# Causal mask by select instead of by product, one normalization for two heads, and output products moved by one slot in a fused attention and feed-forward kernel

## The chip, the cores and the metric

One core of a Trainium2 chip runs the whole program. The metric is the device time of one execution in microseconds (us); less is better. The engines work side by side, each through its own instructions in the order written: TensorE (PE in the profile; PEld its weight loads), VectorE (DVE), ScalarE (ACT), GpSimd (POOL), and SyncE (SP), which only issues transfers.

## What is computed

Attention over 8 batches of 8 heads, 576 positions, 64 values a head, with a causal mask and a bias from a running sum, and then a feed-forward layer on the 4608 rows of 512.

```python
scores = (q @ k.T) / sqrt(64)
s_pos = maximum(s, 0); cum = cumsum(s_pos)
bias = -(cum[query] - cum[key])
scores = where(key > query, -1e9, scores + minimum(bias, 0))
attn = exp(scores - max); attn = attn / (sum(attn) + 1e-9)
x = attn @ v                            # heads side by side: 4608 x 512
h = x @ w_in                            # 512 x 2048
out = (h * clip(h + 3, 0, 6) / 6) @ w_out   # 2048 x 512
```

## The kernel before

**Pairs and slots.** The 64 heads go by in 32 pairs, numbered from 0; four pairs (PPB) make a batch. One turn of the loop over `p` (L847) is called a slot here. For each head, `scores` makes three banks of 512 scores, keys on partitions: g = 0 holds the four blocks on the diagonal, g = 1 and 2 the blocks off it, and `corner` holds the last 64 keys of both heads. ScalarE takes the exponential of each bank into P and PC (L422, L462). `av` multiplies P with v in two parts: part 0 five blocks off the diagonal, part 1 the rest, ten products; v has a column of ones, so that column 64 of the result is the sum. `norm` takes the reciprocal of that column (L503) and multiplies (L504), which makes the head's half of x. `transpose_x` transposes x on TensorE (L518) and VectorE copies it to xT (L523); from pair 8 on, but for one pair and the last, a transfer does this.

**Operands ahead.** In slot p, `get(0)` and `get(1)` transpose q and k of pair p + 1 on TensorE (L253, L266) into a bank each and copy them into the pair's qk tile, by even and odd positions. Of k, ScalarE copies a part and VectorE the rest (L292, L310). For pairs 3 to 6 (`mixed`) q is kept in another order within blocks of 64, and x is put right by a permuted identity. Rows 64 to 67 of a qk tile hold the terms of the bias, loaded by `load_aug` (L162). Four qk tiles take turns.

**The mask.** For pairs 0 to 7 (NPROD) a product of an identity and a matrix of large negative values (L377; L441 in `corner`) starts the bank. For pairs 8 on, GpSimd sets what lies above the diagonal to zero after the exponential (`shut_out`, L426), and 60 more rows of the qk tile (68 to 127, a coarse staircase) keep the exponentials there in range; they are copied from `stair_sb` by GpSimd (`set_stair`, L695) in slots 5 to 7, and by ScalarE in slots 8 and 9 for the fourth tile.

**The feed-forward layer.** `m1` makes h (L547), ScalarE and VectorE make the activation from it (L562, L563), and `m2` makes the output (L574), which VectorE scales (L590). `group` issues one piece of this, four matmuls of 512 columns; a written plan says which through slots 4 to 16 or so, rules after that. It starts in slot 4, when the first batch's x is there. Its weights are loaded by GpSimd in four and eight pieces (L170, L178) from slot 2 to 7.

**Banks.** Eight banks: two for scores, two for h (used for scores too in the first batch), one `o` for the products of head 0, two `po` that are shared by products of head 1, transposes of k and x, and later the output, and one `t` for the transposes of q and k.

**What sets the order.** The schedule is written by hand: each engine takes its instructions in the order in which the code issues them. In slots 0 to 3 the order is scores (p, 0, g = 0 and 1), q of the next pair, scores g = 2, corner, products and norm of (p - 1, head 1), k of the next pair, two banks of head 1 and products part 0 of head 0, the third bank, `transpose_x(p - 1)`, products part 1, norm of (p, head 0). From slot 4 on groups stand between these. GpSimd's queue has in each slot loads, casts of v (L206, L207), selects and copies, one after the other; SP's has the loads of v and later the transposing transfers.

Of the kernel before, what the change touches and what calls it, by code (L numbers as in the profile page):

```python
# [18 lines left out]
def kernel(  # L19
# [31 lines left out]
    VW = 66  # L51
    NROW = 1
    NWARM = (11, 2, 6)
    HALVES = (slice(0, 288), slice(288, SEQ))
# [3 lines left out]

    grp = (np.arange(128) * 61 // 128)[None, :]
    steps_r = np.arange(1, 61)[:, None]  # L60
    stair = np.zeros((128, 2, 128), np.float32)
    stair[68:, 0] = np.where(grp < steps_r, 1.0, 0.0)
    stair[68:, 1] = np.where(grp == steps_r, NEG_BIG, 0.0)
    stair_dram = nc.inline_tensor(stair.astype(np.float16), name="stair")

# [28 lines left out]
    ident2 = keep("ident2", [128, 128], F16)  # L94
    stair_sb = keep("stair_sb", [128, 2, 128], F16)
    bias3 = keep("bias3", [128, 1], F32)
# [62 lines left out]
    def load_aug(p, eng):  # L159
        for hh in range(2):  # L160
# [49 lines left out]
    early = [True]  # L210
    turn = [0]

    def s_bank(shape, name):
# [209 lines left out]

    def shut_out(ap, w):
        part = ap.rearrange("p (t c) -> p t c", c=w)
        nc.gpsimd.affine_select(  # L426
            out=part,
            in_=part,
            pattern=[[0, part.shape[1]], [1, w]],
            compare_op=ALU.is_ge,  # L430
            fill=0.0,
            base=0,
            channel_multiplier=-1,
        )

    def corner(p):
        S = s_bank([128, 2, 64], "Sc")
        by_product = p < NPROD
        rows = slice(0, 68 if by_product else 128)
        if by_product:  # L440
# [29 lines left out]
    def av(p, hh, part):  # L470
        va, pt = vas[p % NVA], Pof(p, hh)
        if part == 0:

            tag = "o" if not hh or NPROD - 1 <= p < NPE - 2 else "po" if p < NPROD else "t"
            O[p, hh] = psum.tile(
                [128, 5, 65], F32, tag=tag, bufs=2 if tag == "po" else 1, name="O"
            )
        o = O[p, hh]
# [11 lines left out]
        else:  # L490
# [5 lines left out]
            block(4, 4, PCs[p % 2][:, c : c + 128], start=False, stop=True)  # L496

    def norm(p, hh):
        o = O.pop((p, hh))
        if hh == 0:  # L500
            X[p] = work.tile([128, 5, 2, D], F16, tag="x", name="x")
        rl = work.tile([128, 5, 1], F32, tag="rl", name="rl")
        nc.vector.reciprocal(out=rl, in_=o[:, :, 64:65])  # L503
        nc.vector.tensor_tensor(  # L504
            out=X[p][:, :, hh, :],
            in0=o[:, :, 0:64],
            in1=rl.to_broadcast([128, 5, 64]),
            op=ALU.mult,
        )
# [182 lines left out]

    def set_stair(i, copy, heads=(0, 1)):
        for hh in heads:
            copy(  # L695
                out=qks[i][64:128, hh, :, 64 * hh : 64 * hh + 640].rearrange(
                    "p i (t c) -> p i t c", c=128
                ),
                in_=stair_sb[64:128, :, None, :].to_broadcast([64, 2, 5, 128]),
            )  # L700

    fill(nc.vector, xT[:, 0, 0:SEQ], 0.0)

    def warm(n):
        W = psum.tile([128, 512], F32, tag="o", name="W")
# [125 lines left out]
    load_v(1, nc.sync)  # L831
    load_aug(2, nc.sync)
    cast_v(0)
    for i in range(2):
# [12 lines left out]
    for p in range(NP):  # L847
# [39 lines left out]
        def pool_end():  # L887
            if p >= NPROD:
                shut_out(PCs[p % 2][:, 0:128], 64)
                shut_out(Pof(p, 1)[:, 0:512], 128)  # L890
            if p >= NPROD and p != 9 and p + 2 < NP:
                if p == 14:
                    cum6(1, nc.gpsimd, whole)
                load_aug(p + 2, nc.gpsimd)

        if p >= PPB:
            for fn, c in {
                4: ((I, 2),),
                5: ((I, 3),),
                6: ((U, 0), (U, 1), (U, 2), (U, 3)),  # L900
                7: ((U, 4), (U, 5), (U, 6), (U, 7)),
            }.get(p, ()):
                fn(c)
        if PPB <= p < NPROD:
            pool_mid()
            if p == 4:
                load_aug(7, nc.gpsimd)
            elif p in (6, 7):
                load_aug(p + 2, nc.gpsimd)
# [6 lines left out]
        if p == 2:  # L916
            nc.sync.dma_start(out=stair_sb, in_=stair_dram.ap())
        if p == 10:
# [12 lines left out]
        if p < PPB:  # L931
            scores(p, 0, 0)
            scores(p, 0, 1)
            get(0)
            scores(p, 0, 2)
            corner(p)
            if p:
                av(p - 1, 1, 0)
                av(p - 1, 1, 1)
                norm(p - 1, 1)  # L940
            get(1)
            scores(p, 1, 0)
            scores(p, 1, 1)
            av(p, 0, 0)
            scores(p, 1, 2)
            if p:
                transpose_x(p - 1)
            av(p, 0, 1)
            norm(p, 0)
            continue  # L950

        if p == PPB:
            early[0] = False
            scores(p, 0, 0)
            av(p - 1, 1, 0)
            av(p - 1, 1, 1)
# [11 lines left out]
        else:  # L968
            scores(p, 0, 0)
            if p >= NPROD:  # L970
                pool_mid()
            get(0)
            group()
            scores(p, 0, 1)
# [10 lines left out]
        corner(p)  # L985
        if p in (8, 9):
            set_stair(3, nc.scalar.copy, (p - 8,))
        elif p == 11:
            new_sum()
            cum1(1, whole)  # L990
# [6 lines left out]
        scores(p, 1, 0)  # L997
        if p >= NPROD:
            pool_end()
        if PPB < p < NPE - 1:  # L1000
# [64 lines left out]
```

## Time and profile before

| | |
|---|---|
| median of 3 runs | 355.29 us (354.62 to 932.81) |
| the profiled execution | 354.79 us, of which the profile's span is 353.1 us |
| TensorE busy | 345.1 us (98%), 2926 matmuls |
| VectorE busy | 230.2 us (65%) |
| ScalarE busy | 224.7 us (64%) |
| GpSimd busy | 169.7 us (48%) |
| mean granted clock of TensorE | 1.00 |
| transfers | 48.35 MB, 137 GB/s over the span |
| mask products: L377 at 512 columns, 16 | 379 ns each |
| select: L426 at 512 columns, 48 | 651 ns each |
| normalization: L503, L504, 64 each | 186 and 492 ns each |

A line of the timeline gives the start and the length in us from the start of the span, the engine, the line of the code, the operation, what it writes and reads, its shape and how many equal ones were merged; in brackets stands how long the engine was idle before it and what ended that. A matmul's length counts from its start to the landing of its result, so that lengths of matmuls in a row overlap; the distance of their starts tells what each costs.

### The profile page before, as it was taken

The numbers are of one execution on the slowest core, as the hardware profiler recorded it, in microseconds if no ns is written. First come the engines' busy times: TensorE is split into PE (matmuls) and PEld (weight loads), VectorE is DVE, ScalarE is ACT, GpSimd is POOL, SyncE is SP. The second block draws the span as 40 slices with busy tenths as digits, with TensorE's granted clock in tenths as the row PEclk, the third lists the DMA queues.
The fourth block names the chain that finished last, engine by engine and source line by source line (L and its number), as shares of the span: only waits on it lengthen the run. The fifth ranks groups of instructions, "written<-read, shape, count | busy, mean of one in ns | idle before, by whom it ended". The sixth has DMA issues, their size and how long they took to land.

```text
span 353.1 us, 7778 instructions
## 1 busy us (share of the span) xinstructions
PE 345.1 (98%) x2926; PEld 191.0 (54%) x2926; DVE 230.2 (65%) x476; ACT 224.7 (64%) x397; POOL 169.7 (48%) x296
## 2 busy tenths in 40 slices
PE   8999999999999999999999999999999999999995
PEld 3775666555555555555555555555555444444442
DVE  7996997676868677666666666757654544544531
ACT  6987896787787667666776666666664334443310
POOL 8977799676778656455555555555310000000000
PEclk9999999999999999999999999999999999999999
DMA  9999999999999999998798959997120100101112
GB/s 164 152 208 209 199 185 182 117 181 196 154 136 100 190 219 188 173 211 186 168 167 198 179 144 197 181 180 164 38 75 14 59 29 34 59 2 59 59 50 72
DMA packets 144782, 48.35 MB, mean 137 GB/s; under 512 B 130648, under 2 KB 139784, under 8 KB 144744
## 3 DMA queue, kind: packets, MB, share of 16 engines
q1 hardware_dynamic: 117112, 37.54, 54.0%
q0 software_dynamic: 27392, 10.03, 24.8%
q8 instruction: 23, 0.38, 0.4%
q10 hardware_dynamic: 240, 0.28, 0.2%
q14 instruction: 15, 0.12, 0.1%
HBM read 37.36 MB, written 9.44 MB: 133 GB/s over the span
## 4 chain that ended last, share of the span: by engine, by line
PE 90%; DVE 4%; ACT 3%; issue 1%; DMA 1%; ACTq 0%
PE po L574 35%; PE ph L547 34%; PE O L481 7%; PE S L403 7%; PE S L388 4%; DVE qk L310 1%; PE pt L266 1%; ACT P L422 1%; DMA s_all<-in_s_dram 1%; DVE x L504 1%; PE ptx L518 1%; PE Sc L454 1%; ACT tr L562 1%; PE S L377 1%; DVE qk L332 1%
## 5 line engine op out<-in xcount | busy, mean ns | idle before, releaser
L563 DVE SCALAR_TENSOR_TENSOR gT<-tr,ph 128x512 f16<-128x512 f32 x144 | 98.9, 687 | 97.6 <-ACT tr L562 96.5
L547 PE MATMUL ph<-xT,w_in_sb 128*128 128x512 f16 x576 | 148.1, 379 | 0.0
L574 PE MATMUL po<-w_out_sb,gT 128*128 128x512 f16 x576 | 145.9, 379 | 0.0
L562 ACT ACTIVATE tr<-ph,bias 128x512 f32<-128x512 f32 x144 | 99.0, 688 | 73.0 <-PE ph L547 70.6
L422 ACT ACTIVATE P<-S 128x512 f16<-128x512 f32 x192 | 111.3, 595 | 37.5 <-PE S L388 22.3
L547 PEld LDWEIGHTS <-w_in_sb 128*128 128x128 f16 x576 | 51.4, 97 | 44.2
L574 PEld LDWEIGHTS <-gT 128*128 128x128 f16 x576 | 50.0, 97 | 46.5 <-issue 0.2
L426 POOL TENSOR_SCALAR_AFFINE_SELECT P<-P 128x512 f16<-128x512 f16 x48 | 31.3, 651 | 44.4 <-ACT P L422 44.4
L403 PE MATMUL S<-qk 68*128 68x448 f16 (+3 forms) x256 | 49.0, 272 | 0.5 <-ACT P L422 0.5
L481 PE MATMUL O<-va,P 128*128 128x65 f16 x896 | 47.9, 193 | 0.3 <-ACT P L422 0.3
L481 PEld LDWEIGHTS <-P 128*128 128x128 f16 x896 | 39.2, 97 | 14.0 <-ACT P L422 0.5
L230 DVE COPY qk<-jt 64x768 f16<-64x768 f16 x84 | 36.8, 439 | 1.2
L403 PEld LDWEIGHTS <-qk 68*128 68x128 f16 x256 | 23.7, 98 | 24.5 <-issue 0.9
L162 POOL DMA_DIRECT2D qk<-rows_of x56 | 32.8, 588 | 1.1 <-PE S L403 0.3
L504 DVE TENSOR_TENSOR x<-O,rl 128x320 f16<-128x320 f32 x64 | 31.5, 492 | 2.2
L590 DVE TENSOR_SCALAR ob<-po 128x512 f32<-128x512 f32 (+1 forms) x36 | 24.3, 676 | 8.3 <-PE po L574 7.6
L388 PEld LDWEIGHTS <-qk 128*128 128x128 f16 (+1 forms) x256 | 18.9, 97 | 14.0 <-DVE qk L310 1.7
L426 POOL TENSOR_SCALAR_AFFINE_SELECT PC<-PC 128x128 f16<-128x128 f16 x24 | 7.0, 293 | 39.9 <-ACT PC L462 39.8
L388 PE MATMUL S<-qk 128*128 128x128 f16 (+1 forms) x256 | 24.8, 219 | 1.0 <-DVE qk L332 0.5
L206 POOL CAST va<-vraw 128x512 f16<-128x512 f32 x32 | 21.0, 656 | 4.7 <-DMA vraw<-in_v_dram 2.4
L310 DVE COPY qk<-pt 64x576 f16<-64x576 f16 x22 | 17.6, 805 | 6.2 <-ACT qk L310 5.9
L202 POOL CAST tok<-raw 128x576 f16<-128x576 f32 x28 | 18.0, 679 | 0.0
(79 smaller groups left out, 201.9 us busy)
## 6 DMA issues: line engine op xcount, KB each, us to landing
out_dram<-ob SPq DMA_DIRECT2D x35, 256.0 KB, 2.0
vraw<-in_v_dram SPq DMA_DIRECT2D x64, 128.0 KB, 4.0
raw<-in_q_dram SPq DMA_DIRECT2D x14, 288.0 KB
raw<-in_k_dram SPq DMA_DIRECT2D x14, 288.0 KB
tok<-in_q_dram POOLq DMA_DIRECT2D x18, 144.0 KB, 5.2
tok<-in_k_dram POOLq DMA_DIRECT2D x18, 144.0 KB, 5.9
w_in_sb<-in_moe_w_in_dram POOLq DMA_DIRECT2D x4, 512.0 KB, 8.5
w_out_sb<-in_moe_w_out_dram POOLq DMA_DIRECT2D x8, 256.0 KB, 7.1
```

What stands on the lines that cost most here:

```text
L162: eng.dma_start(out=qks[p % NQK][64:68, hh, :, 64 * hh : 64 * hh + SEQ], in_=rows_of[g // 32].rearrange("(r g) i t -> g r i t", g=32)[g % ...
L230: copies[par](out=qk[0:64, :, i, 128 * par : 128 * par + 256 * n].rearrange("p h (s two c) -> p h s two c", two=2, c=128)[:, :, :, 0, :], ...
L388: mm(S[:, c], lhsT=kT[rows, c], rhs=qT[rows, c], start=(j == 0 and not by_product), stop=(j == 3 and p >= NROW),)
L403: mm(S[:, c : c + w], lhsT=kT[0:68, 128 * j : 128 * (j + 1)], rhs=qT[0:68, 128 * (j + 1) : SEQ], start=(c == 0), stop=(c != 0 and p >= NROW),)
L422: nc.scalar.activation(out=pt[:, c], in_=S, func=AF.Exp, scale=0.125)
L426: nc.gpsimd.affine_select(out=part, in_=part, pattern=[[0, part.shape[1]], [1, w]], compare_op=ALU.is_ge, fill=0.0, base=0, channel_multip ...
L481: mm(o[:, i, :], lhsT=lhsT, rhs=va[:, hh, j, 0:65], **kw)
L504: nc.vector.tensor_tensor(out=X[p][:, :, hh, :], in0=o[:, :, 0:64], in1=rl.to_broadcast([128, 5, 64]), op=ALU.mult,)
L547: mm(ph, lhsT=w_in_sb[:, kc, ft * 128 : (ft + 1) * 128], rhs=xT[:, kc, n * 512 : (n + 1) * 512], start=(kc == 0), stop=(kc == NKC - 1),)
L562: nc.scalar.activation(out=tr, in_=ph, func=AF.Relu, bias=bias3[:, 0:1])
L563: nc.vector.scalar_tensor_tensor(out=gTs[n][:, ft, :], in0=tr, scalar=6.0, in1=ph, op0=ALU.min, op1=ALU.mult)
L574: mm(po, lhsT=gTs[n][:, ft, t4 * 128 : (t4 + 1) * 128], rhs=w_out_sb[:, ft, :], start=(ft == 0), stop=(ft == NFT - 1),)
```

## The change

Five things are changed together.

1. The mask is a product only for pairs 0 to 3 (NMASK = 4). From pair 4 on GpSimd selects; for the mixed pairs with a pattern of the same order. `pool_mid` and `pool_end`, which issue the selects, now run in all slots from 4 on, after the scores they read.
2. The staircase has 7 rows instead of 60, with steps of 16, and is loaded straight into rows 68 to 74 of the qk tile by SP (`load_stair`, seven loads for pairs 4 to 10). `set_stair` and its copies are gone.
3. Products of heads 0 and 1 go to a tile of two adjacent banks, `OO`, and for pairs 0 to 2 and 4 to 6 one reciprocal of 128x10 and one multiplication of 128x640 (`norm_pair`) take the place of two of each. In the first batch the products of head 0 of a pair move from the end of its own slot into the next one, and `get(1)` moves ahead of the products of head 1. The tile `po` has one bank; the output takes turns between it and the second bank of `OO`. The transposes of x use bank `t`, but for pair 3.
4. q of pairs 7 to 10 is copied in two parts with a group between them.
5. The pieces of the weights are issued after the select and the cast of v, two of w_out already in slot 5 and three in slots 6 and 7 (before: four in slots 6 and 7). Loads of bias rows for pairs 7 to 9 go from GpSimd's queue to SP's.

```diff
+    NMASK = PPB
+    NSTAIR = 7
...
+    def load_stair(p, eng):
+        eng.dma_start(
+            out=qks[p % NQK][68 : 68 + NSTAIR], in_=stair_drams[mixed(p, 0)].ap()
+        )
...
+    OO = psum.tile([128, 2, 512], F32, tag="oo", name="OO")
+
+    def paired(p):
+        return p < PPB - 1 or PPB <= p < NPROD - 1
...
     def t_bank(other, name):
         if not done[2] and other:
-            return psum.tile([128, 640], F16, tag="po", bufs=2, name=name)
+            return psum.tile([128, 640], F16, tag="po", name=name)
         return psum.tile([128, 640], F16, tag="t", name=name)
...
-        by_product = p < NPROD
+        by_product = p < NMASK
         if g == 0:
-            rows = slice(0, 68 if by_product else 128)
+            rows = slice(0, 68 if by_product else 68 + NSTAIR)
...
-    def shut_out(ap, w):
+    def shut_out(p, ap, w):
         part = ap.rearrange("p (t c) -> p t c", c=w)
+        pattern = [[0, part.shape[1]], [1, w]]
+        if mixed(p, 0):
+            part = part.rearrange("p t (g w v) -> p t g w v", w=4, v=16)
+            pattern = [[0, part.shape[1]], [64, w // 64], [1, 4], [4, 16]]
+            if w == 64:
+                part, pattern = part[:, :, 0], [pattern[0]] + pattern[2:]
...
-            tag = "o" if not hh or NPROD - 1 <= p < NPE - 2 else "po" if p < NPROD else "t"
-            O[p, hh] = psum.tile(
-                [128, 5, 65], F32, tag=tag, bufs=2 if tag == "po" else 1, name="O"
-            )
+            if hh and p >= NPE - 2:
+                O[p, hh] = psum.tile([128, 5, 65], F32, tag="t", name="O")
+            else:
+                half = hh if p < NPROD - 1 else 0
+                O[p, hh] = OO[:, half, 0:325].rearrange("p (i c) -> p i c", c=65)
...
+    def norm_pair(p):
+        o = OO[:, :, 0:325].rearrange("p h (i c) -> p h i c", c=65)
+        X[p] = work.tile([128, 5, 2, D], F16, tag="x", name="x")
+        rl = work.tile([128, 2, 5, 1], F32, tag="rl2", name="rl2")
+        nc.vector.reciprocal(out=rl, in_=o[:, :, :, 64:65])
+        nc.vector.tensor_tensor(
+            out=X[p].rearrange("p i h d -> p h i d"),
+            in0=o[:, :, :, 0:64],
+            in1=rl.to_broadcast([128, 2, 5, 64]),
+            op=ALU.mult,
+        )
+
     def norm(p, hh):
+        if paired(p):
+            if hh:
+                norm_pair(p)
+            return
...
-        pt = t_bank(True, "ptx")
+        pt = t_bank(p == PPB - 1, "ptx")
...
         if fq == 0:
-            po = psum.tile([128, 512], F32, tag="po", bufs=2, name="po")
+            if len(pos) % 2:
+                po = OO[:, 1]
+            else:
+                po = psum.tile([128, 512], F32, tag="po", name="po")
...
         def pool_mid():
-            if p >= NPROD:
-                shut_out(Pof(p, 0)[:, 0:512], 128)
+            shut_out(p, Pof(p, 0)[:, 0:512], 128)
             if nxt:
                 cast_v(p + 1)
-            if p in (5, 6, 7):
-                set_stair((p + 3) % NQK, nc.gpsimd.tensor_copy)
+            for fn, c in {
+                4: ((I, 2),),
+                5: ((I, 3), (U, 0), (U, 1)),
+                6: ((U, 2), (U, 3), (U, 4)),
+                7: ((U, 5), (U, 6), (U, 7)),
+            }.get(p, ()):
+                fn(c)
...
             scores(p, 0, 1)
             get(0)
+            if p:
+                av(p - 1, 0, 0)
+                av(p - 1, 0, 1)
             scores(p, 0, 2)
             corner(p)
+            get(1)
             if p:
                 av(p - 1, 1, 0)
                 av(p - 1, 1, 1)
                 norm(p - 1, 1)
-            get(1)
             scores(p, 1, 0)
             scores(p, 1, 1)
-            av(p, 0, 0)
             scores(p, 1, 2)
             if p:
                 transpose_x(p - 1)
-            av(p, 0, 1)
-            norm(p, 0)
+            if p == PPB - 1:
+                av(p, 0, 0)
+                av(p, 0, 1)
+                norm(p, 0)
             continue
...
             scores(p, 0, 0)
-            if p >= NPROD:
-                pool_mid()
-            get(0)
-            group()
+            pool_mid()
+            if NPROD - 1 <= p + 1 < NPE:
+                pt = transpose_in(p + 1, 0)
+                transpose_out(p + 1, 0, pt, pars=(0,))
+                group()
+                transpose_out(p + 1, 0, pt, pars=(1,))
+            else:
+                get(0)
+                group()
...
-        if p in (8, 9):
-            set_stair(3, nc.scalar.copy, (p - 8,))
```

More of the change, by code (lines that the diff above doesn't have):

```diff
@@ L52 @@
     NROW = 1
+    NMASK = PPB
+    NSTAIR = 7
     NWARM = (11, 2, 6)
     HALVES = (slice(0, 288), slice(288, SEQ))
[L59 to L64, printed above, removed]
+    grp = (np.arange(128) // 16)[None, :]
+    steps_r = np.arange(1, NSTAIR + 1)[:, None]
+    under = np.where(grp < steps_r, 1.0, 0.0)
+    equal = np.where(grp == steps_r, NEG_BIG, 0.0)
+    over = under.reshape(NSTAIR, 2, 16, 4).transpose(0, 1, 3, 2).reshape(NSTAIR, 128)
+    stair_drams = []
+    for name, of_q in (("stair", under), ("stairm", over)):
+        stair = np.zeros((NSTAIR, 2, 2, SPAD), np.float16)
+        for hh in range(2):
+            for i, rows in enumerate((of_q, equal)):
+                stair[:, hh, i, 64 * hh : 64 * hh + 640] = np.tile(rows, (1, 5))
+        stair_drams.append(nc.inline_tensor(stair, name=name))
     cpool = ctx.enter_context(tc.tile_pool(name="consts", bufs=1))
@@ L94 @@
     ident2 = keep("ident2", [128, 128], F16)
-    stair_sb = keep("stair_sb", [128, 2, 128], F16)
     bias3 = keep("bias3", [128, 1], F32)
@@ L428, in shut_out @@
             in_=part,
-            pattern=[[0, part.shape[1]], [1, w]],
+            pattern=pattern,
             compare_op=ALU.is_ge,
@@ L437, in corner @@
         S = s_bank([128, 2, 64], "Sc")
-        by_product = p < NPROD
-        rows = slice(0, 68 if by_product else 128)
+        by_product = p < NMASK
+        rows = slice(0, 68 if by_product else 68 + NSTAIR)
         if by_product:
@@ L691 @@
     nc.gpsimd.tensor_copy(out=unmix(perm), in_=mix(ident))
[L693 to L700, printed above, removed]
     fill(nc.vector, xT[:, 0, 0:SEQ], 0.0)
     def warm(n):
-        W = psum.tile([128, 512], F32, tag="o", name="W")
+        W = OO[:, 0]
         for _ in range(n):
@@ L832 @@
     load_aug(2, nc.sync)
+    load_stair(PPB, nc.sync)
     cast_v(0)
@@ L887, in pool_end @@
         def pool_end():
-            if p >= NPROD:
-                shut_out(PCs[p % 2][:, 0:128], 64)
-                shut_out(Pof(p, 1)[:, 0:512], 128)
+            shut_out(p, PCs[p % 2][:, 0:128], 64)
+            shut_out(p, Pof(p, 1)[:, 0:512], 128)
             if p >= NPROD and p != 9 and p + 2 < NP:
@@ L893, in pool_end @@
                     cum6(1, nc.gpsimd, whole)
[L894 to L904, printed above, removed]
-            pool_mid()
-            if p == 4:
-                load_aug(7, nc.gpsimd)
-            elif p in (6, 7):
                 load_aug(p + 2, nc.gpsimd)
@@ L916 @@
         if p == 2:
-            nc.sync.dma_start(out=stair_sb, in_=stair_dram.ap())
+            for i in range(PPB + 1, NPROD):
+                load_stair(i, nc.sync)
+        if p in (4, 6, 7):
+            n = 7 if p == 4 else p + 2
+            if p != 4:
+                load_stair(n, nc.sync)
+            load_aug(n, nc.sync)
+        elif p == 8:
+            load_stair(10, nc.sync)
         if p == 10:
@@ L969 @@
             scores(p, 0, 0)
-            if p >= NPROD:
-                pool_mid()
-            get(0)
-            group()
+            pool_mid()
+            if NPROD - 1 <= p + 1 < NPE:
[6 more added lines that the diff above has]
+                group()
             scores(p, 0, 1)
@@ L985 @@
         corner(p)
-        if p in (8, 9):
-            set_stair(3, nc.scalar.copy, (p - 8,))
-        elif p == 11:
+        if p == 11:
             new_sum()
@@ L997 @@
         scores(p, 1, 0)
-        if p >= NPROD:
-            pool_end()
+        pool_end()
         if PPB < p < NPE - 1:
```

## The prediction

> **What bounds the kernel now.** I count pairs of heads from 0 as the code does; a slot is one turn of the loop over p. First the busy shares on the page: TensorE has nearly all of the span.
>
> ```profile
> PE 345.1 (98%) x2926; PEld 191.0 (54%) x2926; DVE 230.2 (65%) x476; ACT 224.7 (64%) x397; POOL 169.7 (48%) x296
> ```
>
> Matmuls overlap, so that share can hide waits; the starts in the timeline of TensorE cannot. From 34 us on, each matmul starts where the one before leaves off (512 columns every 0.216 us: groups of four, 0.86 apart), and I find less than 1.2 us of lost time in all of 34 to 350 us. There an instruction taken from TensorE is worth its pitch, and one added costs it. Before 34 us it is different. The timeline of TensorE at the starts of slots 2 and 3:
>
> ```profile
> 17.14 0.45 PE L518 MATMUL ptx<-ident,x 128*128 128x128 f16 x5 [0.39 <-DVE x L504]
> ...
> 17.74 0.38 PE L377 MATMUL S<-shut,ident 128*128 128x512 f16 x1
> 18.34 0.40 PE L388 MATMUL S<-qk 68*128 68x128 f16 x4 [0.22 <-DVE qk L310]
> ...
> 21.73 0.38 PE L377 MATMUL S<-shut,ident 128*128 128x512 f16 x1
> 22.16 0.40 PE L388 MATMUL S<-qk 68*128 68x128 f16 x4
> ...
> 25.55 0.38 PE L377 MATMUL S<-shut,ident 128*128 128x512 f16 x1
> 26.13 0.40 PE L388 MATMUL S<-qk 68*128 68x128 f16 x4 [0.20 <-DVE qk L310]
> ```
>
> Each pair's first scores (L388) start when the last copy of its k is written: a loop from pair to pair, of 4.55, 3.82 and 3.97 us (13.79, 18.34, 22.16, 26.13). The loop of slot 2 can be read on ScalarE and then VectorE:
>
> ```profile
> 18.84 1.57 ACT L422 ACTIVATE P<-S 128x512 f16<-128x512 f32 x3 [1.00 <-PE S L388]
> 20.29 0.30 ACT L462 ACTIVATE PC<-Sc 128x128 f16<-128x128 f32 x1
> 20.44 0.81 ACT L310 COPY qk<-pt 64x576 f16<-64x576 f16 x1
> ```
> ```profile
> 20.26 0.20 DVE L503 RECIPROCAL rl<-O 128x5 f32<-128x5 f32 x1
> 20.49 0.49 DVE L504 TENSOR_TENSOR x<-O,rl 128x320 f16<-128x320 f32 x1
> 21.29 0.81 DVE L310 COPY qk<-pt 64x576 f16<-64x576 f16 x1 [0.31 <-ACT qk L310]
> 22.13 0.46 DVE L523 COPY xT<-ptx 128x576 f16<-128x576 f16 x1
> ```
>
> Scores at 18.34, first exponential 0.50 later, three of them and the corner's, then ScalarE's half of the k copy, and only when that ends (21.25) VectorE's half, to 22.10; scores at 22.16. The normalization at 20.26 to 20.98 costs nothing here: VectorE does it while it waits for ScalarE.
>
> **Part 1: products a slot later, one normalization (pairs 0 to 2).** In the new order of VectorE the k copies of a slot come ahead of the normalization, since the transposes of k are now issued before the last products; and at the end of the slot TensorE transposes x ahead of the next pair's mask and scores, in one queue. So the loop gets longer by what used to lie beside it: reciprocal, multiplication of both heads, five transposes and the mask. The multiplication has no row: 128x320 takes 0.492, and the fused step at 128x512 0.687, so 1.02 ns more an element, 0.82 for 640; its bounds are one (0.49) and two (0.98) of the single ones. Start to start of reciprocal and multiplication is 0.22 (18.69 to 18.91); the transposes are 5 x 0.056 = 0.28, the mask 0.22. A start after VectorE ends costs 0.05 (17.09 to 17.14).
>
> Slot 1: pair 1's scores at 13.62 (its k is written at 13.57; before, they also stood behind a product and a mask, 13.79). Exponentials from 14.07; the third waits for its scores, now behind a product of 15 x 0.031, so the corner's ends at 15.85, ScalarE's k copy at 16.33, VectorE's two (0.48 and 0.80) at 17.65, multiplication 17.91 to 18.73, transposes 18.78, mask 19.06, **scores of pair 2 at 19.28** (18.34 before). Slot 2: +0.5 first exponential; the product puts the third 0.13 later; ScalarE's copy 21.45 to 22.26, VectorE's to 23.11, x at 24.18, transposes 24.23, mask 24.51, **pair 3 at 24.73** (22.16). Slot 3: ScalarE's half is the short one (26.90 to 27.38), VectorE's to 28.70, x at 29.77, transposes 29.82, then pair 3's own first product (0.47), no mask, **pair 4 at 30.57** (26.13). That is +4.4 us; with the bounds of the multiplication +3.4 to +4.9. Slot 4 (26.13 to 34.17, 8.04 us) loses 0.27 us of masks, but its second head already waits for an exponential (0.33 before L403 at 32.78), so I give it 7.85. Pair 5 starts at 38.42, **+4.25**.
>
> **Part 2: mask by select.** Eight masks of 512 columns (L377, 0.216) and four corners (L441, 0.055) go: 1.95 us of TensorE. Of these, slot 4's are counted above, and 0.49 a slot remain for pairs 5, 6, 7: 1.46. Part of it is not had, because of the banks: x is now transposed into the bank of the q transposes (there were two others to take turns in). The copy out of it runs late:
>
> ```profile
> 41.35 0.45 DVE L523 COPY xT<-ptx 128x576 f16<-128x576 f16 x1
> ```
>
> It ends at 41.80, behind the k copies and a fused step, and next slot's q transposes started at 41.70; without the masks TensorE is there at about 41.0 and waits to about 41.6, since ScalarE and VectorE come only 0.2 earlier. The same at 48.83 (copy to 48.73). So slots 5 to 7 give 0.6 of 1.46 (bounds 0 and 1.46). The selects go to POOL: 0.65 for 512 columns, 0.29 for the corner, and for the mixed order of pairs 4 to 6 by the two L679 rows (0.29 plain, 0.34 mixed) up to 0.76. POOL's slot 5 is then two q/k issues 1.3, two selects 1.3 to 1.5, casts 0.9, three weight issues 2.25, corner 0.3: 6.0 to 6.3 in 6.6 to 7.1. The select of the corner, behind the weight issues, ends about 43.6; TensorE wants it at 44.7. So nothing, with 1.1 us of room.
>
> **Part 3: what else moves.** The staircase copies go (POOL 6 x 1.25, ScalarE 2 x 1.25); seven small loads on SP (0.58 to issue) take their place, issued a pair or more ahead, three of them with no reader to wait for; six pair-row loads go from POOL (0.59 each) to SP behind the v loads. SP's issues wait for places 8 loads back, and v lands 9 to 12 us after issue at 27 to 31 us; v of pair 7, issued about 33, is there by 46, and its cast is due at 47. Weights now stand behind select and cast: the last w_in at 41.1, landing within 10.1 (33.51 to 43.63 before) for use at 52.8; the last w_out at 56, landing 63.5 for use at 68.8. No stall, but the room falls to 1.5 us. ScalarE without its copies in slots 8 and 9, and q copies split around a group in slots 6 to 9, can save what TensorE lost there, 0.4 at 71.4 us and little more: **-0.4** (0 to -0.5). From slot 10 on, product and output banks alternate as before: 0.
>
> **Sum.** 4.25 - 0.6 - 0.4 = +3.25 on a span of 353.1. The profiled execution took 354.79, 1.7 outside the span, so **358.0**; the median of the runs shown is 355.29, of which this is +0.8%. With all bounds (3.2 to 4.7; 0 to -1.46; 0 to -0.5; POOL 0 to +0.5) 356.0 to 360.0.
>
> **The clock.** TensorE loses up to 1.9 us at a time in slots 1 to 3. In this trace it idled 0.7 us at 8.6 to 9.3 without the granted clock leaving 1.00; the 11 warming matmuls ran at 0.43 a start. [...]
>
> **Rivals.** A, faster: the loop of the first batch does not close over x, because VectorE reaches the normalization while TensorE is still busy; then the waits of before (0.55, 0.38, 0.20, 0.36 at the starts of slots) go with the masks: 354.8 - 1.95 - up to 1.5, so 351.3 to 353. For it: VectorE is busy only 3.6 of 4 us a slot there. Against: in its order the k copies come first and wait for ScalarE. It decides if x is ready by 3.4 us into slot 2. B, slower still: POOL becomes the one that ends last in slots 4 to 7. Its cast waited 2.24 us for a v load at 36.55; such a wait now stands ahead of weights and selects, and beyond 1.1 us of room each us costs one, three times over: 358 + 1 to 4, 359 to 362. Against: the v loads are issued early relative to the later slots. C: the granted clock halves in the first batch, as in the warming matmuls (0.43 against 0.216); 3.6 us of work a slot becomes 7.2, +5: 363 or more. D, the edits of the later slots do nothing: within the sum, 358.4.
>
> **Chances.** Forecast with D 0.67, A 0.17, B 0.12, C 0.04. Range 352.5 to 361.5: the whole of the forecast's own, more than half of A, most of B. About 2% (7 us) is what a measurement of this kernel can tell from no change. Faster by more than that (under 348.2) 0.02: the masks and all waits together are worth 5; slower (over 362.4) 0.06, from C and the end of B; within, 0.92.
>
> **What would show it.** Right: first scores of pairs 2, 3, 4 near 19.3, 24.7, 30.6; before them TensorE idle on the transposes of x, released by the new multiplication of about 0.8; k copies ahead of it, released by ScalarE; q transposes of pair 7 waiting for the copy of x; no wait of TensorE for a select. Wrong: transposes of x without a wait (A), products released by a select (B), a clock under 1.00 (C), or a multiplication far from 0.8.

## The result and the profile after

The changed kernel takes **401.49 us** (median of 4 runs, 400.32 to 403.44) beside 355.03 of the kernel before on the same chip: 1.132 times as long, with an interval of 1.125 to 1.139. The prediction had 358.0 and a range to 361.5. The profiled execution took 400.32 us, with a span of 398.6 (before 353.1).

TensorE is busy for 88% of the span, from 98%, with 12 matmuls fewer. Its line on the page of the changed kernel:

```profile
PE 349.8 (88%) x2914; PEld 193.2 (48%) x2914; DVE 227.5 (57%) x464; ACT 222.1 (56%) x395; POOL 164.7 (41%) x296
```

What TensorE waits for is in the table of waits of the changed kernel: its columns are the waiting engine, tile and line, what it waited for, us in all, how often, and the longest:

```profile
PE OO L615 <- DVE x L542: 33.6, 19, 1.8
...
PE ptx L556 <- DVE x L525: 5.7, 3, 2.0
```

**The first row is the loss.** It is a matmul of the output (L615, `m2`) that waits for a normalization (L542). The timelines of TensorE and of VectorE near the end of a slot in the long even part of the kernel:

```profile
176.90 0.44 PE L503 MATMUL OO<-va,P 128*128 128x65 f16 x9
177.18 0.19 PE L503 MATMUL OO<-va,PC 128*128 128x65 f16 x1
179.19 1.02 PE L615 MATMUL OO<-w_out_sb,gT 128*128 128x512 f16 x4 [1.82 <-DVE x L542]
```
```profile
177.82 0.69 DVE L601 SCALAR_TENSOR_TENSOR gT<-tr,ph 128x512 f16<-128x512 f32 x1 [1.63 <-ACT tr L600]
178.42 0.19 DVE L541 RECIPROCAL rl<-OO 128x5 f32<-128x5 f32 x1
178.64 0.49 DVE L542 TENSOR_TENSOR x<-OO,rl 128x320 f16<-128x320 f32 x1
```

The products of head 0 end in the first half of OO; the output then starts in the second half, and does so only when VectorE has read the first. The same place of the kernel before, on TensorE and on VectorE:

```profile
157.19 0.19 PE L481 MATMUL O<-va,PC 128*128 128x65 f16 x1
157.22 1.03 PE L574 MATMUL po<-w_out_sb,gT 128*128 128x512 f16 x4
```
```profile
158.44 0.19 DVE L503 RECIPROCAL rl<-O 128x5 f32<-128x5 f32 x1
158.66 0.49 DVE L504 TENSOR_TENSOR x<-O,rl 128x320 f16<-128x320 f32 x1
```

There the output starts 0.03 us after the last product, and the normalization ends 1.9 us later, in nobody's way. After the change the distance of these starts is 2.01 us (177.18 to 179.19), 1.98 more than before. This wait of 1.98 us comes 18 times, from pair 18 on in every pair: there the first scores of a pair come every 11.21 us instead of every 9.22. Taking at each place how much later the group starts than the matmul ahead of it lets it, I get 36.7 us in all.

**The first batch.** First scores of pairs 2, 3 and 4 at 19.37, 25.43 and 32.55 (before 18.34, 22.16, 26.13). TensorE, and VectorE in slot 2:

```profile
18.86 0.45 PE L556 MATMUL ptx<-ident,x 128*128 128x128 f16 x5 [1.93 <-DVE x L525]
...
24.50 0.72 PE L556 MATMUL ptx<-ident,x 128*128 128x128 f16 x5 [1.82 <-DVE x L525]
...
31.79 0.45 PE L556 MATMUL ptx<-ident,x 128*128 128x128 f16 x5 [1.99 <-DVE x L525]
```
```profile
22.53 0.80 DVE L326 COPY qk<-pt 64x576 f16<-64x576 f16 x1 [1.29 <-ACT qk L326]
23.36 0.22 DVE L524 RECIPROCAL rl<-OO 128x10 f32<-128x10 f32 x1
23.61 0.82 DVE L525 TENSOR_TENSOR x<-OO,rl 128x640 f16<-128x640 f32 x1
```

This is the predicted loop: ScalarE's half of the k copy, VectorE's half, the normalization, the transposes of x. But at 24.50 five transposes take 0.72 instead of 0.45. The table of stretches says why; its columns are the stretch and its length, the busy time (and count) of TensorE, its weight loads, VectorE, ScalarE and GpSimd, then the granted clock, the transfers' share and GB/s:

```profile
21.00:24.40 3.40, 1.68 (x33) 1.19 (x29) 2.04 (x4) 2.86 (x6) 2.40 (x4) 1.00 1.26 214
24.40:27.80 3.40, 3.30 (x34) 2.75 (x35) 1.27 (x4) 1.08 (x2) 1.24 (x3) 0.50 1.57 149
```

For 3.4 us the granted clock was a half. In the kernel before it was 1.00 from 4.9 us to the end of the work, at 353.0.

**Slots 5 to 7.** The waits of TensorE at 44 to 64 us:

```profile
48.72 0.42 PE L282 MATMUL pt<-ident,tok 96*128 96x96 f16 x6 [0.43 <-DVE xT L561]
...
59.59 0.42 PE L282 MATMUL pt<-ident,tok 96*128 96x96 f16 x6 [0.20 <-DVE qk L326]
62.13 0.44 PE L556 MATMUL ptx<-perm,x 128*128 128x128 f16 x5 [0.88 <-DVE qk L326]
```

The first, the transposes of q behind the copy of x in the one bank t, was predicted, and so was its like in the next slot (about 0.6 each; by the distance of starts 0.59 and 0.47). The last two are in slot 7 and were not: k of pair 8 goes through bank t too, behind q's copy, which is now split, and x waits behind k.

### The profile page after: what moved, and what is told of

The parts are those of the page before. It is cut to its first block, busy times and chain, and to the rows that moved or that the text cites. A ratio compares the mean times of both kernels' runs of the same rounds, so it can differ in the third digit from the quotient of the medians.

```text
span 398.6 us, 7759 instructions
## 1 busy us (share of the span) xinstructions
PE 349.8 (88%) x2914; PEld 193.2 (48%) x2914; DVE 227.5 (57%) x464; ACT 222.1 (56%) x395; POOL 164.7 (41%) x296
## 4 chain that ended last, share of the span: by engine, by line
PE 72%; DVE 10%; ACT 7%; issue 5%; POOL 2%; DMA 2%; SPq 1%; ACTq 0%; POOLq 0%
PE ph L585 26%; PE OO L615 15%; PE po L615 14%; PE S L419 5%; ACT tr L600 4%; PE S L404 3%; DVE x L542 3%; PE O L503 2%; DVE qk L326 2%; PE OO L503 2%; PE OO L739 2%; ACT P L438 1%; DMA s_all<-in_s_dram 1%; DVE gT L601 1%; DVE rl L541 1%
## 5 line engine op out<-in xcount | busy, mean ns | idle before, releaser
L615 PE MATMUL OO<-w_out_sb,gT 128*128 128x512 f16 x288 | 73.9, 378 | 33.6 <-DVE x L542 33.6
L615 PEld LDWEIGHTS <-gT 128*128 128x128 f16 x576 | 51.3, 97 | 81.9 <-issue 35.6
L615 PE MATMUL po<-w_out_sb,gT 128*128 128x512 f16 x288 | 73.9, 379 | 0.0
L448 POOL TENSOR_SCALAR_AFFINE_SELECT P<-P 128x512 f16<-128x512 f16 x56 | 37.0, 661 | 87.1 <-ACT P L438 87.0
L246 DVE COPY qk<-jt 64x768 f16<-64x768 f16 x84 | 34.3, 409 | 1.2
L503 PE MATMUL OO<-va,P 128*128 128x65 f16 x574 | 30.2, 194 | 2.0 <-DVE ob L631 1.0
L169 POOL DMA_DIRECT2D qk<-rows_of x50 | 29.7, 597 | 1.6 <-issue 1.0
L448 POOL TENSOR_SCALAR_AFFINE_SELECT PC<-PC 128x128 f16<-128x128 f16 x28 | 8.4, 301 | 50.8 <-ACT PC L484 50.7
L404 PE MATMUL S<-qk 75*128 75x128 f16 (+1 forms) x256 | 25.1, 220 | 0.1
L404 PEld LDWEIGHTS <-qk 75*128 75x128 f16 (+1 forms) x256 | 19.1, 98 | 12.0 <-DVE qk L326 0.5
L503 PE MATMUL O<-va,P 128*128 128x65 f16 x322 | 17.3, 193 | 0.0
```

The source lines that it names most:

```text
L169: eng.dma_start(out=qks[p % NQK][64:68, hh, :, 64 * hh : 64 * hh + SEQ], in_=rows_of[g // 32].rearrange("(r g) i t -> g r i t", g=32)[g % ...
L246: copies[par](out=qk[0:64, :, i, 128 * par : 128 * par + 256 * n].rearrange("p h (s two c) -> p h s two c", two=2, c=128)[:, :, :, 0, :], ...
L404: mm(S[:, c], lhsT=kT[rows, c], rhs=qT[rows, c], start=(j == 0 and not by_product), stop=(j == 3 and p >= NROW),)
L448: nc.gpsimd.affine_select(out=part, in_=part, pattern=pattern, compare_op=ALU.is_ge, fill=0.0, base=0, channel_multiplier=-1,)
L503: mm(o[:, i, :], lhsT=lhsT, rhs=va[:, hh, j, 0:65], **kw)
L615: mm(po, lhsT=gTs[n][:, ft, t4 * 128 : (t4 + 1) * 128], rhs=w_out_sb[:, ft, :], start=(ft == 0), stop=(ft == NFT - 1),)
```

## The experiments

**Theory 1**: the program keeps its dependencies for the tile, not for the bank, so a wait crosses from one half of OO to the other. **Theory 2**: the order in the first batch makes a longer loop. **Theory 3**: the clock falls after a stretch in which TensorE was idle for half. The rivals: one po bank instead of two, or the selects on GpSimd, make the steady loss. Times are medians; a ratio is to the kernel before on the same chip (354.7 to 354.8 us).

### Two tiles of one bank

```diff
-    OO = psum.tile([128, 2, 512], F32, tag="oo", name="OO")
+    OO = [psum.tile([128, 512], F32, tag=f"oo{i}", name=f"OO{i}") for i in range(2)]
...
-        if paired(p):
-            if hh:
-                norm_pair(p)
+        if paired(p) and not hh:
             return
+        for h in (0, 1) if paired(p) else (hh,):
+            norm_one(p, h)
```

> The changed kernel with its two-bank tile OO cut into two tiles of one bank, and the pair's normalization done as two single ones at the same place; all else as changed. Theory 1 (dependencies are kept per tile, so that the output's last group waits for a normalization that reads the other bank): the 36.7 us of those waits go, and two more of about 1 us each across the banks; the single normalizations cost 0.16 us more in each of three slots. Time 359 to 363 us, first scores of pair 31 within 2 us of 9.22 a pair after pair 17. Rival 1 (the steady loss comes from a single po bank, or from the new order on GpSimd): the loss of 2 us a pair stays, 390 us or more. In both, first scores of pairs 2, 3, 4 stay near 19.4, 25.4, 32.5.

Measured: 364.11 us, 1 above the range, ratio 1.026 (1.023 to 1.029); **37.4 us less** than the changed kernel. The output's group in OO on its page (busy, mean ns, then the idle time before it):

```profile
L605 PE MATMUL OO<-w_out_sb,gT 128*128 128x512 f16 x288 | 73.9, 378 | 0.0
```

No idle time, from 33.6. From pair 19 on a pair takes 9.23 us. The same matmuls write one bank for the products and another for the output, as before; what differs there is only the tile that the banks belong to (the normalization as two instructions is found in six pairs, all ahead of pair 7). Rival 1 falls: the single po bank and GpSimd's order are as in the changed kernel.

### The shared tile alone, in the kernel before

```diff
+    OO = psum.tile([128, 2, 512], F32, tag="oo", name="OO")
...
-            po = psum.tile([128, 512], F32, tag="po", bufs=2, name="po")
+            if len(pos) % 2:
+                po = OO[:, 1]
+            else:
+                po = psum.tile([128, 512], F32, tag="po", name="po")
```

The products go to OO[:, 0] and OO[:, 1] as in the change.

> The kernel before, with nothing changed but the banks: o and one of the po banks become the two halves of one tile, and the other po bank is alone. Theory 1: the wait of 1.98 us a pair comes here too, from slot 7 to 10 on, so 18 to 22 times: 355 + 36 to 44 = 391 to 399 us. Rival 1: the shared tile alone does nothing, 355 to 358 us (what a single bank for transposes of k and x may cost before 60 us).

Measured: 402.45 us, ratio 1.136 (1.133 to 1.138), as slow as the whole change and more than expected. Its page has the changed kernel's row again:

```profile
L579 PE MATMUL OO<-w_out_sb,gT 128*128 128x512 f16 x288 | 73.8, 378 | 33.6 <-DVE x L506 33.6
...
L579 PE MATMUL po<-w_out_sb,gT 128*128 128x512 f16 x288 | 73.9, 379 | 1.7 <-DVE xT L525 1.7
```

36.9 us by the distance of starts, as theory 1 has it. The rest (some 11 us) is what my sum lacked: with po single, the transposes of x wait for k's copies (3.9 us in five waits), an output waits for x in po (the second row), and products in OO wait for the copy of an output in the other half. Since the kernel with two tiles has the same single po bank without that row, the one part that is enough for the loss is the shared tile.

### The first batch in the old order

```diff
             get(0)
-            if p:
-                av(p - 1, 0, 0)
-                av(p - 1, 0, 1)
...
-            get(1)
             if p:
                 av(p - 1, 1, 0)
                 av(p - 1, 1, 1)
                 norm(p - 1, 1)
+            get(1)
...
+            av(p, 0, 0)
```

From the kernel with two tiles.

> As the first of these (two tiles of one bank), and the first batch in the order of before: products and normalization in their old slot, transposes of x behind them. Theory 2 (the first batch's order lengthens the loop from pair to pair): first scores of pairs 2, 3, 4 back to 18.3, 22.2, 26.2; 4.4 us of loop and about 2 of the lower clock less than with the new order, so 353.5 to 356.5 us, and the granted clock 1.00 throughout. Rival 2 (what the first batch loses is made good later by less waiting): within 2 us of the kernel with the new order.

Measured: 357.47 us, 356.28 to 361.19, ratio 1.009 (1.006 to 1.012): 6.6 less than the new order with two tiles; first scores of pairs 2 to 4 at 18.44, 22.25 and 26.21. Theory 2 holds in place and size, though the time is 1 us above its range. The long executions show something else, and in them the granted clock does not stay at 1.00, as the expectation had it (in the profile 0.50 from 37.8 to 41.3 us). The profiled one took 360.79; its TensorE, and its GpSimd ahead of the wait:

```profile
36.92 0.20 PE L503 MATMUL OO<-va,PC 128*128 128x65 f16 x1 [2.54 <-DMA tok<-in_k_dram]
```
```profile
33.62 0.61 POOL L218 CAST va<-vraw 128x512 f16<-128x512 f32 x1 [2.09 <-DMA vraw<-in_v_dram]
...
36.50 0.36 POOL L448 TENSOR_SCALAR_AFFINE_SELECT PC<-PC 128x128 f16<-128x128 f16 x1
```

The releaser named on TensorE is a transfer, but the product with PC starts where the select of the corner ends: that select stood behind two casts, which waited for v (2.09 and 1.02), and a weight load. This is rival B of the prediction, in place and mechanism. With the new order of the first batch it does not show, most likely because v then has 6 us more to arrive: in the changed kernel the cast of this slot, at 34.53, starts without a wait.

### Normalization first, products a slot later

Only `get(1)` is moved back behind the normalization (the lower half of the diff above), from the kernel with two tiles.

> As the kernel with two tiles of one bank, but in slots 1 to 3 the transposes of k are issued behind the last products and the normalization, so that VectorE has the normalization ahead of its k copies; the products of head 0 stay a slot later. Theory 2a (the loop closes over x only because the k copies stand ahead of the normalization on VectorE): the waits of 2.2 to 2.4 us before the transposes of x go, first scores of pairs 2, 3, 4 near 18.8, 23.2, 27.6, clock 1.00, 358 to 360.5 us. Rival 2a (the products a slot later are what lengthens the loop): pair 4 stays at 31.5 or later, 362 us or more.

Measured: 357.66 us, 357.52 to 357.75, a little better than expected, ratio 1.008 (1.007 to 1.010); first scores at 18.85, 23.01 and 27.50. So 6.45 us of the change's loss hang on one line, the place of k's transposes. VectorE in slot 2 now:

```profile
21.60 0.49 DVE L532 TENSOR_TENSOR x<-OO,rl 128x320 f16<-128x320 f32 x1
22.14 0.81 DVE L326 COPY qk<-pt 64x576 f16<-64x576 f16 x1
```

x is ready before the k copy, at a time when VectorE would wait for ScalarE anyway. By medians the products a slot later cost nothing beside the old order (357.47). But the long executions are in that median: pair 4 comes 1.3 us later here (27.50 beside 26.21), and the shortest executions of the old order take 356.3.

### Matmuls that keep TensorE busy

```diff
+                W = s_bank([128, 512], "Wf")
+                for _ in range(7):
+                    mm(W, lhsT=ident, rhs=shut[:, None, :].to_broadcast([128, 4, 128]), start=True, stop=True)
                 transpose_x(p - 1)
```

From the kernel with two tiles, whose first-batch waits are 2.2 to 2.4 us and whose clock was 0.50 from 31.4 to 34.8.

> As the kernel with two tiles of one bank, with seven matmuls more of 512 columns (1.5 us) ahead of the transposes of x in slots 1 to 3, into a bank nobody reads: TensorE waits there 2.2 to 2.4 us in any case. Theory 3 (the granted clock falls to a half for 3.4 us after a stretch of 3.4 us of which TensorE was idle for half, 1.76 us or more, here in the order of 2.4): idle falls to 0.9, clock 1.00 throughout, and the 1 to 1.7 us that the half clock cost are won: 362.2 to 363.2 us. Rival 3 (the clock falls for another reason, a schedule or the load of the transfers): it still falls to 0.50 between 24 and 42 us, and the time is 364 us or, by the added work, more.

Measured: 361.85 us, ratio 1.020 (1.019 to 1.022): **more work, 2.3 us less time**, a little more than expected. The kernel with two tiles, in the stretch where its clock is a half (columns as above):

```profile
31.40:34.80 3.40, 3.40 (x42) 2.85 (x42) 1.83 (x5) 0.60 (x1) 1.42 (x3) 0.50 1.14 192
```

With the matmuls added, the stretches that were shown of the changed kernel:

```profile
21.00:24.40 3.40, 3.20 (x40) 1.86 (x36) 2.02 (x6) 2.86 (x6) 2.06 (x4) 1.00 1.26 205
24.40:27.80 3.40, 3.04 (x61) 2.67 (x62) 1.67 (x4) 1.93 (x5) 1.39 (x2) 1.00 1.34 194
```

The clock is 1.00 in both, and its mean over the span is 1.000, with the transfers as dense as before (205 and 194 GB/s), so rival 3 falls. From pair 0's first scores to pair 5's it is 30.43 us, beside 31.85 in the profile with two tiles. The rest of the 2.3 fits the other executions with two tiles: the mean granted clocks of the four are 0.995, 0.995, 0.991 and 0.986, which is one to three stretches at a half (an estimate from these means), where the four with the added matmuls have 0.998 or more. What the fall hangs on is taken up in the last section; theory 3's "idle for half" does not decide it.

### The mask alone

The kernel before with select from pair 4 on, the staircase by seven-row loads, and the moved weight and bias loads; its banks and orders otherwise.

> The kernel before with only the mask changed: select from pair 4 on, seven staircase rows by transfers, the weight and bias loads on their new queues; banks, normalizations, order of the first batch and q copies as before. By the prediction's step for the masks 1.95 us of TensorE go, and with two banks for transposes no wait for the copy of x takes them back: 352.8 to 354.3 us. Rival (GpSimd late in slots 4 to 7, with selects of 0.87 us): a wait of TensorE for a select or a weight load, 355.5 to 359 us.

Measured: 355.24 us, 354.33 to 357.14, ratio 1.002 (1.000 to 1.004). No gain, though TensorE has 1.95 us less to do; the time lies between the two ranges. Its waits:

```profile
34.92 0.20 PE L498 MATMUL O<-va,PC 128*128 128x65 f16 x1 [0.43 <-DMA tok<-in_k_dram]
45.97 1.02 PE L564 MATMUL ph<-xT,w_in_sb 128*128 128x512 f16 x4 [0.41 <-DVE gT L580]
...
62.11 0.59 PE L591 MATMUL po<-w_out_sb,gT 128*128 128x512 f16 x2 [0.58 <-DMA w_out_sb<-in_moe_w_out_dram]
```

The first is GpSimd's (the corner's select). The last is for a piece of w_out that GpSimd issued behind its selects, at 51.42; the kernel before issued it no earlier (51.05), but there it landed after 6.6 us, here after 10.6. The one between is VectorE's (h's bank is not read yet), with another of 0.30 in the next slot.

### The same without the selects

```diff
     def shut_out(p, ap, w):
+        if p < NPROD:
+            return
```

> The kernel with the select alone, with the selects of slots 4 to 7 left out (nothing masks the diagonal of pairs 4 to 7): GpSimd has 2.1 us less in each of these slots, all else is the same. Theory 4 (the masks' 1.95 us are not won because GpSimd is full and its casts and weight loads come late): 352.8 to 353.8 us. Rival 4 (VectorE and ScalarE, at 0.9 or more of these slots, take the time back): no change, 354.7 to 355.6 us, with TensorE waiting for the banks of h.

Measured: 354.30 us, 354.15 to 356.23, ratio 1.000 (0.999 to 1.001), 0.9 less than with the selects: the wait for the corner's select is gone, and so is the one for w_out, whose piece is issued at 49.18 now (and lands after 10.6 us as well); the two on VectorE (0.39 and 0.30) are still there. Neither theory has it whole. By the medians GpSimd's selects take about 0.9 of the 1.95, VectorE and the rest about 0.6, and 0.4 is left; but the intervals of the two kernels touch, and this one's holds 1.000, so the split is an estimate.

### Select and split q copies; the cast last

The first adds the split q copies to the kernel with the mask alone. The second moves GpSimd's casts of v behind the selects in slots 4 to 7.

> The kernel before with the mask by select and the q copies split around a group; banks, normalizations and the first batch as before. Beside the kernel with the select alone (355.24) it tells what the split costs or saves: by the prediction 0 to 0.5 us saved, 354.7 to 355.3; if the k transposes of pair 8, which use the bank of q, wait for the late q copy, 0.4 us more: 355.6. Beside the kernel with two tiles and the old first batch (357.47) it tells what the banks alone cost: 1.5 to 2.5 us.

> The kernel with the select and the split q copies (355.56), and on GpSimd in slots 4 to 7 the casts of v, which wait for a load, moved behind the weight loads and the three selects. Theory 4b (the executions of that kernel above 354 us are those in which a late v holds the cast and with it the corner's select and the weights): the spread falls, 353.9 to 354.6 us, at or just under the kernel before. Rival 4b (the cast then comes late itself, or the spread comes from elsewhere): median 355.2 us or more, with the same spread of 3 us.

Measured: 355.56 us (353.93 to 356.96), ratio 1.002 (1.000 to 1.004); with the cast last 354.73 (353.85 to 356.74), ratio 1.001 (0.999 to 1.003). The split saves nothing beside the select alone; k of pair 8 waits for the late half of q, 0.60 us in the profile. The wait for the corner's select is in neither profile, but the spread of 3 us is as wide with the cast last, so what makes it stays open, and neither kernel is faster than the one before. Beside the 357.47 of the two tiles, the banks cost 1.9 us by medians, as expected.

### The pair's tile kept, with other writers

```diff
+                if p < NPROD - 1:
+                    bank = OO[:, hh]
+                else:
+                    bank = psum.tile([128, 512], F32, tag="po", name="O")
...
-            if len(pos) % 2:
-                po = OO[:, 1]
-            else:
-                po = psum.tile([128, 512], F32, tag="po", name="po")
+            po = OO[:, len(pos) % 2]
```

> The changed kernel with its two-bank tile and its one normalization for both heads kept, and two moves: from pair 7 on the products go to the single bank po and the output takes turns on the two halves of OO; in slots 1 to 3 the transposes of k are issued behind the normalization. Theory 1b (a shared tile costs only where a late reader of the other half stands before a writer: here the only readers of OO are the copies of the output, which are done a group of h before the next output begins): the steady loss goes as with two tiles, 356.5 to 358.5 us beside the 357.66 of two tiles in the same order. Rival 1b (any two banks in one tile cost some 2 us a pair in this schedule): 385 us or more.

Measured: 366.46 us, ratio 1.033 (1.031 to 1.034). The steady 2 us a pair are gone (a pair takes 9.23 and 9.48 in turn), but it is 8.8 us above the two tiles, and I had expected none. TensorE:

```profile
282.26 1.02 PE L615 MATMUL OO<-w_out_sb,gT 128*128 128x512 f16 x4 [0.37 <-DVE ob L631]
...
360.12 1.02 PE L615 MATMUL OO<-w_out_sb,gT 128*128 128x512 f16 x4 [0.78 <-DVE ob L631]
```

Where an output follows on the last one with less than a copy's time (0.68) between, it waits for the copy out of the other half: 0.25 every second pair, 0.53 once the attention is over, 0.94 at the very end; 9.4 us in all. The mechanism is theory 1's, and its price is the distance from the reader's end to the writer's turn; that outputs follow so closely was not in my expectation.

### x through the bank po

```diff
-        pt = t_bank(p == PPB - 1, "ptx")
+        pt = t_bank(True, "ptx")
```

From the kernel with two tiles and the normalization first.

> The kernel with two tiles and the normalization first (357.66), with x transposed into the bank po of the k transposes instead of the bank t of the q transposes. Prediction's step on the banks (q transposes wait about 0.6 us for the copy of x): the waits at the starts of slots 6 and 7 (0.60 and 0.53) and the one of 1.31 us in slot 7, behind the split q copy, go; 355.2 to 356.2 us. Rival 5 (one bank for k and x is no better: k waits for x or x for k): within 0.5 us of 357.66.

Measured: 364.46 us, ratio 1.026 (1.023 to 1.028): 6.8 us worse, the opposite of what I expected, and worse than rival 5 too. Its waits in slots 5 to 7:

```profile
44.98 0.45 PE L546 MATMUL ptx<-perm,x 128*128 128x128 f16 x5 [1.25 <-DVE qk L326]
...
62.69 1.09 PE L605 MATMUL po<-w_out_sb,gT 128*128 128x512 f16 x4 [1.95 <-DVE xT L551]
```

x now waits for k's copies, which are later than q's, in the first batch too, where the clock fell to 0.50 again (19.1 to 22.6); behind the wait of 1.95 it fell a second time: the matmuls at 63.58 take 0.63 instead of 0.38, and the mean granted clock of 0.991 over 363.1 us is two such stretches, by an estimate from that mean. What the change took away is the second po bank; of the two banks left, t is the better one for x.

Both edits together, the pair's tile with other writers and x through po, were to keep all parts of the change at 354.8 to 356.2 us. That order of instructions cannot run: its waits close in a circle (a deadlock). So no kernel here keeps the whole change without its loss.

## Why the prediction was wrong

Where 46.5 us went, by differences of medians (from several chips, so they add to 46.8): the shared tile 37.4 (401.49 to 364.11); the place of k's transposes 6.45 (to 357.66), of which the filling matmuls alone win back 2.3; the rest 2.95. In the profile of that last kernel pair 4 comes 1.4 us later than before (27.50 beside 26.13), pair 7 1.2 (49.77 beside 48.61), since the masks that went pay for the wait of 0.60 in slot 6, and pair 8 3.1 (60.35 beside 57.26), with waits of 0.54, 0.36 and 1.32 in slot 7 (by the distance of starts).

- **The step that failed** is "From slot 10 on, product and output banks alternate as before: 0". The banks do alternate as before. That the waits go with them was taken for granted; with both in one tile the program's waits are for the tile. It cost 37 us, against a sum of 3.25. No rival had it either: A, B and C looked at the first 70 us, D took the later edits to do nothing, and the one edit with an effect in most of the later slots was priced in one sentence. The profile had what was needed: the normalization of head 0 (158.44) stands 1.2 us behind the start of the output in the next bank (157.22).
- **First batch.** The loop is the predicted one, step for step: pair 2 at 19.37 (19.28 predicted), pair 3 at 25.43 (24.73), the multiplication 0.82 (0.82), released by ScalarE as said. Pair 4 came at 32.55 instead of 30.57. About 1 us of that difference is the clock's: slots 2 and 3 took 6.06 and 7.12, and with the clock at 1.00, in the kernel with filling matmuls, 5.89 and 6.31. The rest is the sum's, which had 5.45 and 5.84; what it lacks there stays open. Slot 4 then took 8.70 instead of 7.85: the wait across the halves again, when products follow a normalization (0.75 at 33.52; with two tiles there is none).
- **The clock.** The sum let it at 1.00 through waits of up to 1.9 us. No run shows that for the first batch: in the trace of before, the longest that TensorE stood idle from 4.9 us on is 0.68 (by the distance of starts), and in the changed kernel the clock fell to 0.50 at 24.4, in the second of three such waits (1.93, 1.82 and 1.99). Rival C had the event, at 0.04 and at 5 us; in the profiled execution one stretch of 3.4 us came, worth about 1 before pair 4. The two longest executions (403.44 and 402.58) have mean clocks of 0.983 and 0.987, where the profiled one has 0.996: three or four such stretches, by an estimate from these means. The event was named; what failed is the assumption that the clock stays at 1.00 through these waits.
- **Mask.** The waits for the copy of x came as predicted, 0.59 and 0.47. The select in mixed order takes 0.86 to 0.90, above the 0.76 I had as its bound, so GpSimd's slot is fuller. No wait for a select came in the changed kernel, as forecast; with a quick first batch it does, and the mask alone is then worth nothing (ratio 1.000 to 1.004), the lower bound of the sum's 0.6 (0 to 1.46).
- **Other moves.** -0.4 was predicted; slot 7 lost 1.4 (0.37 and 1.04) by k of pair 8 and x behind the split q copy, which the sum had as a saving. That single bank was in the sum only for q.

## What to carry to other kernels

Two banks in one tile are one thing to every wait: before joining tiles for the sake of one wide instruction, list for each writer of either half the last reader of the other half, and read in the timeline when it ends; here one instruction for two, 0.3 us of VectorE in each of six pairs, cost 37 us. An edit whose effect repeats in every slot deserves more of the working than all those of the first slots together. When copies are in one queue with the normalization, what waits for another engine goes last, and the piece that is ready goes into the gap.

## What the hardware showed that was not expected

**The clock fell after stretches that were far from idle.** In five of these profiles the granted clock fell to 0.50 in the first 45 us, each time for 3.41 us, and with x in po a second time at about 63.5. In a stretch of that length before each fall, TensorE was idle (by the distance of starts) for 1.9 us in the changed kernel, 2.4 with two tiles, 2.6 with the old first batch, 1.8 with the shared tile alone, and 2.1 both times with x in po; no single wait was over 2.7. With the shared tile alone no wait was over 1 us there (0.76 and 0.65 in its timeline), and the clock fell.

But idle time does not decide it. The changed kernel again, at one of the waits of 1.98 us, and the stretch behind it:

```profile
92.66:96.07 3.41, 1.59 (x19) 0.92 (x17) 1.83 (x5) 0.72 (x2) 1.86 (x2) 1.00 1.21 92
96.07:99.50 3.43, 3.43 (x36) 1.98 (x33) 1.53 (x4) 2.37 (x4) 1.43 (x3) 1.00 1.78 178
```

TensorE is busy for 1.59 us here, less than the 1.68 before the fall, and the clock stays at 1.00; waits of 1.98 us come 18 times in this profile, and from 27.8 us to the end of the span it is 1.00. The work is of another kind: here mostly 512 columns at a time with weights on all 128 rows, in the first batch scores with weights on 68 rows and products of 65 columns. No run tests whether that makes the difference, so why the clock falls stays open.

**A wait can shorten the program by being filled.** Seven matmuls for nothing, 1.5 us three times over in a time in which TensorE waited anyway, took 2.3 us off the median: the work behind them ran at a granted clock of 1.00, where it had run at 0.50.
